# First block of attention: weights left unnormalised, the value product turned round with a ones column, rows scaled, one identity product

## The chip, the cores and the metric

The kernel runs on one core of a Trainium2 chip. The metric is the device time of one execution in microseconds (us). Each core has TensorE (PE in the profile; its weight loads are PEld), VectorE (DVE), ScalarE (ACT), GpSimd (POOL) and SyncE (SP), which issues the transfers. Every engine works through its own instructions in the order in which they were written. SBUF is the working memory, PSUM the memory that TensorE writes its products to.

## What is computed

Sliding-window attention with a linear position bias on 4 batches of 8 heads, 576 positions and 64 elements per head, and behind it two expert layers on the 2304 rows that come out:

```python
scores = scale * np.matmul(q, k.transpose(0, 1, 3, 2))
mask = (rel >= 0) & (rel < window)          # window = 128
scores = np.where(mask, scores + bias[None], -1000000000.0)
scores = scores - np.max(scores, axis=-1, keepdims=True)
attn = np.exp(scores)
attn = attn / (np.sum(attn, axis=-1, keepdims=True) + 1e-09)
attn_out = np.matmul(attn, v)
h = x @ w_in                                 # x: attn_out, 2304 x 512
x = (h * np.clip(h + 3.0, 0.0, 6.0) / 6.0) @ w_out
xn = x / rms * rms_g
out = (silu(xn @ w_gate) * (xn @ w_val)) @ w_out2
```

## The kernel before

The 2304 rows are 18 tiles of 128 rows, taken in six blocks of three. Attention for a block is done two heads at a time: a *pair* is two heads (128 columns of the 512), and a *step* is one pair and one tile of 128 query rows. Block 0 has four pairs of three steps, 12 steps in all. Its attention runs first, on its own, in the loop `for t in range(AHEAD)` (15 turns, called slots below); the attention of the later blocks is woven into the products of the expert layers, and the first three steps of block 1 are begun in slots 12 to 14. Behind the loop comes `product1`, the first product of the first expert layer, with its Relu on ScalarE.

A step consists of these parts, each one slot or more after the one it needs:

- `scores` (S): TensorE, two matmuls (one a head) against up to 256 keys; each float32 matmul shows as two instructions in the trace. The two heads lie on different rows of the array.
- `bias`: VectorE adds the position bias and takes the minimum of each row (the sign is turned), one pass a head.
- `exp`: ScalarE takes the exponential, in `before` with the sum of each row as a second result; GpSimd then adds 1e-9 to the sums and takes the power -1.
- `divide` (D): VectorE multiplies the weights by the reciprocals, one pass a head.
- `transpose` (T): TensorE turns the weights round, 128 keys at a time, into the PSUM tile `ps_t`, which has one buffer. A pair's first step in block 0 has no keys before it and two transposes, the others four.
- `weights`: ScalarE copies `ps_t` to SBUF (`pt`).
- `values` (V): TensorE multiplies with the values as the stationary operand (64 columns, one head) and `pt` as the moving one (128 columns). The heads write to the upper and the lower half of the same PSUM tile `ps_av`, which holds the three steps of a pair and has one buffer.
- `finish`: behind a pair's third step, ScalarE casts `ps_av` into `xs` and VectorE subtracts to get the low part; then the values of the pair two further on are loaded.

`plan` says how many slots behind a pair's first each part of its three steps comes; the table `slots` is filled from it, and the loop takes what `at(t)` gives. The order inside a slot is written out by hand. Between the steps the loop also converts the first two weight tiles from 64-bit words to two 32-bit parts: `W1.step(k, ...)`, whose parts 0, 1 and 4 are ScalarE passes (L131, L136, L145) and 2, 3 and 5 VectorE passes (L140, L143, L147). `prepare` scales the next pair's queries on VectorE and loads the keys and queries of the pair after. Loads are issued by SyncE in the order written.

Of the kernel before, what the change touches and what calls it, by code (L numbers as in the profile page):

```python
# [10 lines left out]
F32 = mybir.dt.float32  # L11
# [4 lines left out]
AF = mybir.ActivationFunctionType  # L16
# [4 lines left out]
P = 128  # L21
# [39 lines left out]
EARLY = {0: 1, 1: 3, 2: 6, 3: 8, M2 - 1: 11}  # L61
PAIRS2 = NTILE // 6

KINDS = "QSDTLV"

OPEN = {"reuse_waits": "tile"}

# [6 lines left out]
def fused_kernel(ctx: ExitStack, tc: tile.TileContext, qd, kd, v, w1, w2, rms_g, out):  # L74
# [201 lines left out]
    class Pair:  # L276
# [17 lines left out]
        def load_v(self):  # L294
            j, k0, nk = self.j, self.lo * P, self.nch * P
            self.vr = ap.tile([P, 4, P], F32, tag="v", name="vraw", bufs=2)
            sp.dma_start(
                out=self.vr[:, : self.nch],
                in_=v[k0 : k0 + nk, j * P : (j + 1) * P].rearrange("(c p) d -> p c d", p=P),
            )  # L300

        def scale(self):
            q = self.qr[:, : self.n * P]
# [26 lines left out]
    class Step:  # L330
# [12 lines left out]
        def scores(self):  # L343
            pr, c0, k0 = self.pair, self.c0, (self.i - 1 - self.pair.lo) * P
            for x, y in PARTS_OF if pr.parts else ():
                for a, s in enumerate(self.s):
                    rows = slice(a * D, (a + 1) * D)
                    pe.matmul(  # L348
                        s[:, c0:],
                        lhsT=pr.qs[rows, x, self.u * P : (self.u + 1) * P],  # L350
                        rhs=pr.ks[rows, y, k0 + c0 : k0 + 2 * P],
                        start=(x == 0 and y == 0),
                        stop=(x == 1),
                    )
            for a, s in enumerate(self.s if not pr.parts else ()):
                rows = slice(a * D, (a + 1) * D)
                pe.matmul(  # L357
                    s[:, c0:],
                    lhsT=pr.qr[rows, self.u * P : (self.u + 1) * P],
                    rhs=pr.kr[rows, k0 + c0 : k0 + 2 * P],  # L360
                    start=True,
                    stop=True,
                )
# [16 lines left out]
                pool.memset(self.t[:, :, :HALF], 0.0)  # L380

        def exp(self):
            self.den = small.tile([P, 2], F32, tag="den", name="den")
            for a in range(2):
                p = self.t[:, a, self.p0 :]
                act.activation(p, p, AF.Exp, bias=self.m[:, a : a + 1], scale=-1.0, accum_out=self.den[:, a : a + 1])  # L386
            self.r = small.tile([P, 2], F32, tag="r", name="r")
            pool.tensor_scalar(self.r, self.den, 1e-9, None, ALU.add)  # L388
            pool.tensor_tensor(self.r, self.r, minus, ALU.pow)  # L389
# [12 lines left out]
        def weights(self):  # L402
# [3 lines left out]
            for c, sign in ((0, -1), (1, 1)) if self.joint else ():  # L406
# [2 lines left out]
                    base=c - 1, pattern=[[0, 2], [sign, P]], channel_multiplier=-sign,  # L409
                )  # L410

        def values(self):
            pr = self.pair
            if pr.acc is None:
                pr.acc = ps_a.tile([P, 3, P], F32, tag="A", name="ps_av")
            for c in range(self.from_, 2):
                for a in range(2):
                    pe.matmul(  # L418
                        pr.acc[a * D : (a + 1) * D, self.u],
                        lhsT=pr.vr[:, self.i - 1 + c - pr.lo, a * D : (a + 1) * D],  # L420
                        rhs=self.pt[:, a, c],
                        start=(c == self.from_),
                        stop=(c == 1),
                        skip_group_check=True,
                    )
# [8 lines left out]
    for k, pr in enumerate(pairs):  # L434
        b, j = divmod(k, H // 2)
        if b < 2:
            t0, plan = 3 * j if b == 0 else AHEAD - 3 + 3 * j, {"S": (0, 1, 2), "D": (1, 2, 3), "T": (2, 3, 4), "V": (3, 4, 5)}
        else:
            t0, plan = AHEAD + M1 * (b - 1) - 2 + 4 * j, {"S": (0, 0, 0), "D": (1, 1, 2), "T": (None, 2, 3), "L": (1, None, None), "V": (5, 5, 5)}
        slots["Q"].setdefault(t0 - (2 if b < 2 else 1), []).append(pr)  # L440
        for u in range(pr.n):
            step = Step(pr, u)
            for kind, at in plan.items():
                if at[u] is not None:
                    slots[kind].setdefault(t0 + at[u], []).append(step)

    def at(t):
        return [slots[kind].get(t, []) for kind in KINDS]

# [125 lines left out]
    busy(WARM)  # L575
    pairs[0].scale()
    for t in range(AHEAD):
        q, s_, d_, t_, _, v_ = at(t)
        scores(s_, t % 2)
        for x in t_:  # L580
            x.transpose()
        for x in v_:
            x.values()
        for x in t_:
            x.weights()
        for x in s_:
            x.bias()
        prepare(q, s_)
        for x in d_:
            x.divide()  # L590
        for x in v_:
            if x.last:
                finish(x.pair)
        for x in s_:
            x.exp()
        if t == 2:
            W1.load(3)
        W1.step(0, *{4: (0,), 5: (1, 2), 7: (3,), 9: (4, 5)}.get(t, ()))
        W1.step(1, *{8: (0,), 11: (1, 2)}.get(t, ()))
# [83 lines left out]
    for p, (b, m0, m1) in enumerate(PARTS):  # L683
# [13 lines left out]
        xs = xs_of[b]  # L697
        for m in range(m0, m1):
            t, slot = slot, slot + 1
            q, s_, d_, t_, l_, v_ = at(t)  # L700
            go = p < 3 or last or (t - AHEAD) % 4 in (0, 3)
            if p == 3 and m == 2:
                first.close()
# [301 lines left out]
```

## Time and profile before

| | before |
|---|---|
| time, median of 3 runs | 956.25 us (955.87 to 956.81) |
| span of the profiled execution | 954.2 us |
| PE busy | 937.7 us (98%) |
| DVE busy | 640.5 us (67%) |
| ACT busy | 454.2 us (48%) |
| POOL busy | 186.3 us (20%) |
| PE tenths in the first four of 40 slices | 7, 8, 9, 9 |
| TensorE clock in the first two slices, tenths of full speed | 8, 9 |

A slice is 23.9 us. The page's chain of work that ended last is 87% PE. The clock is the one that was granted: full is 2.4 GHz, half is 1.2 GHz. In the rows below a group "x4" is four instructions that follow each other; its time is the stretch that they cover, and for a group of one form "mean ns" is that of a single instruction, from its start to its result, so that successive ones overlap.

### The profile page before, as it was taken

The page shows a single profiled execution, that of the slowest core. Times are in us where ns is not written, and L with a number is a line of the kernel's source. Part 1 is how long each engine was busy: PE and PEld are TensorE (multiplying, and loading weights), DVE is VectorE, ACT ScalarE, POOL GpSimd, SP SyncE. Part 2 cuts the span into 40 slices and gives each one's busy share as a digit, 9 for nine tenths or more (in the row PEclk, how much of TensorE's full clock was granted, in tenths as well). Part 3 has the DMA queues.
Part 4 walks back from the last instruction along what each step waited for, and adds up shares of the span by engine and source line. Part 5 has one row for each costly group of instructions (what it writes and reads, how often), then busy time and mean ns, then how long its engine had stood idle before and what let it go on. Part 6 is the DMA issues. An engine that isn't in the chain of part 4 may idle for free.

```text
span 954.2 us, 14654 instructions
## 1 busy us (share of the span) xinstructions
PE 937.7 (98%) x5336; PEld 832.9 (87%) x5336; DVE 640.5 (67%) x1336; ACT 454.2 (48%) x969; POOL 186.3 (20%) x327
## 2 busy tenths in 40 slices
PE   7899999999999999999999999999999999999998
PEld 4587888888888888888899999999999999999996
DVE  5788667555878777877467657777545577545555
ACT  6899566455666655655455453433131323231120
POOL 4333012332223332422124223310000000000000
PEclk8999999999999999999999999999999999999999
DMA  6555401113666555554355757866757555755521
GB/s 231 183 194 194 187 20 51 32 53 117 198 211 203 172 164 174 164 169 130 122 182 210 287 206 293 320 229 234 249 212 281 214 202 199 265 206 211 214 86 67
DMA packets 67432, 175.02 MB, mean 183 GB/s; under 512 B 5024, under 2 KB 41888, under 8 KB 62624
## 3 DMA queue, kind: packets, MB, share of 16 engines
q1 hardware_dynamic: 67360, 174.09, 52.2%
q8 instruction: 42, 0.69, 0.3%
q14 instruction: 30, 0.25, 0.1%
HBM read 130.03 MB, written 44.04 MB: 182 GB/s over the span
## 4 chain that ended last, share of the span: by engine, by line
PE 87%; DVE 6%; ACT 4%; issue 2%; POOL 1%; ACTq 0%; POOLq 0%; DVEq 0%
PE ps_o L497 19%; PE ps_h L484 18%; PE ps_y L892 15%; PE ps_o L845 10%; PE ps_S L845 8%; PE ps_A L845 6%; PE ps_h L845 4%; PE ps_av L418 2%; PE ps_t L400 2%; PE ps_s L357 1%; DVE wx L143 1%; PE ps_s L348 1%; ACT t L386 1%; ACT wx L136 1%; DVE t L371 1%
## 5 line engine op out<-in xcount | busy, mean ns | idle before, releaser
L497 PE MATMUL ps_o<-w,g 128*128 128x512 f32 x864 | 224.0, 402 | 2.1 <-DVE w L147 1.9
L484 PE MATMUL ps_h<-xs,w 128*128 128x384 f32 x1152 | 220.2, 339 | 0.0
L484 PEld LDWEIGHTS ps_h<-xs,w 128*128 128x128 f32 x1152 | 202.4, 188 | 5.8 <-issue 0.2
L497 PEld LDWEIGHTS ps_o<-w,g 128*128 128x128 f32 x864 | 156.2, 188 | 41.1 <-issue 6.3
L892 PE MATMUL ps_y<-wo,g 128*128 128x512 f32 x648 | 150.2, 390 | 0.5 <-DVE g L881 0.5
L892 PEld LDWEIGHTS ps_y<-wo,g 128*128 128x128 f32 x648 | 121.3, 188 | 25.1 <-DVE g L881 0.9
L723 DVE SCALAR_TENSOR_TENSOR t<-t,ps_h 128x384 f32<-128x384 f32 x96 | 53.2, 554 | 98.7 <-ACT t L722 98.6
L722 ACT ACTIVATE t<-ps_h,three 128x384 f32<-128x384 f32 x96 | 55.5, 578 | 84.1 <-PE ps_h L484 80.2
L899 DVE TENSOR_TENSOR y<-y,ps_y 128x512 f32<-128x512 f32 x90 | 61.7, 686 | 35.3 <-PE ps_y L892 35.0
L386 ACT ACTIVATE t<-t,m 128x128 f32<-128x128 f32 (+1 forms) x144 | 61.4, 428 | 29.4 <-DVE t L378 14.2
L728 ACT CAST g<-t 128x384 fp32r<-128x384 f32 x96 | 49.5, 516 | 47.5 <-DVE t L723 46.2
L734 DVE TENSOR_TENSOR g<-t,g 128x384 fp32r<-128x384 f32 x96 | 54.4, 567 | 23.3 <-ACT g L728 23.0
L868 ACT ACTIVATE r<-r 128x384 f32<-128x384 f32 x36 | 19.0, 527 | 105.6 <-DVE r L867 105.6
L845 PE MATMUL ps_o<-S,tw 128*128 128x384 f32 x336 | 66.2, 339 | 0.3 <-DVE t L865 0.3
L388 POOL TENSOR_SCALAR r<-den 128x2 f32<-128x2 f32 x72 | 27.4, 380 | 187.6 <-ACT t L386 186.0
L845 PEld LDWEIGHTS ps_o<-S,tw 128*128 128x128 f32 x336 | 59.3, 188 | 1.4 <-DVE u L856 0.8
L389 POOL TENSOR_TENSOR r<-r,minus 128x2 f32<-128x2 f32 x72 | 56.0, 778 | 6.0
L407 POOL TENSOR_SCALAR_AFFINE_SELECT pt<-pt 128x256 f32<-128x256 f32 x82 | 34.5, 421 | 107.5 <-ACT pt L405 104.5
L853 ACT COPY s<-ps_S 128x384 f32<-128x384 f32 x18 | 8.7, 481 | 86.9 <-PE ps_S L845 86.9
L371 DVE CUSTOM_DVE_ANT_0 t<-ps_s,rel 128x256 f32<-128x256 f32 (+2 forms) x128 | 45.2, 395 | 3.6 <-PE ps_s L357 3.6
L143 DVE SCALAR_TENSOR_TENSOR wx<-wx,wy 128x512 uint32<-128x512 uint32 (+1 forms) x52 | 44.2, 850 | 0.0
L136 ACT ACTIVATE wx<-wraw 128x512 f32<-128x512 f32 (+1 forms) x52 | 42.8, 824 | 0.0
(138 smaller groups left out, 1471.9 us busy)
## 6 DMA issues: line engine op xcount, KB each, us to landing
tw<-t SPq DMA_DIRECT2D x52, 896.0 KB, 6.3
wraw<-w SPq DMA_DIRECT2D x36, 512.0 KB, 4.1
wo<-w SPq DMA_DIRECT2D x18, 1024.0 KB, 4.9
wraw<-w SPq DMA_DIRECT2D x16, 1024.0 KB, 9.1
t<-th SPq DMA_DIRECT2D x12, 896.0 KB, 4.3
t<-tl SPq DMA_DIRECT2D x12, 896.0 KB, 4.3
b<-wx SPq DMA_DIRECT2D x24, 256.0 KB, 2.6
w<-w SPq DMA_DIRECT2D x12, 512.0 KB, 3.0
```

Source lines behind the costliest of these rows:

```text
L143: vec.scalar_tensor_tensor(out=xi, in0=xi, scalar=3, in1=y, op0=ALU.logical_shift_left, op1=ALU.bitwise_or)
L371: vec.tensor_tensor_reduce(out=self.t[:, a, c0:], in0=s[:, c0:], in1=(rel_split if self.i in SPLITS else rel)[:, c0:], scale=2.0 ** (-8.0 ...
L386: act.activation(p, p, AF.Exp, bias=self.m[:, a : a + 1], scale=-1.0, accum_out=self.den[:, a : a + 1])
L389: pool.tensor_tensor(self.r, self.r, minus, ALU.pow)
L484: pe.matmul(ps[:, : n * P], lhsT=w[:, a, c * P : (c + 1) * P], rhs=xs[c][:, b, : n * P], start=(k == 0), stop=(k == 3 * KC - 1),)
L497: pe.matmul(o, lhsT=g[:, a, i * P : (i + 1) * P], rhs=w[:, b], start=(m == first and a == 0 and b == 0), stop=(m == last and a == 1),)
L722: act.activation(r[:, :nq], ps[:, :nq], AF.Relu, bias=three)
L723: vec.scalar_tensor_tensor(out=r[:, :nq], in0=r[:, :nq], scalar=6.0, in1=ps[:, :nq], op0=ALU.min, op1=ALU.mult)
L734: vec.tensor_sub(g[:, 1, :nq], r[:, :nq], f32(g[:, 0, :nq]))
L845: pe.matmul(ps, lhsT=w[a][:, k, c * P : (c + 1) * P], rhs=x[:, b, c], start=(start and j == 0), stop=(j == 5), skip_group_check=True,)
L892: pe.matmul(ps, lhsT=gs[i + k][:, a, t // 3, t % 3 * P : (t % 3 + 1) * P], rhs=wo[i + k][:, b], start=(k == 0 and a == 0 and b == 0), stop ...
L899: vec.tensor_add(acc[t], acc[t], ps)
```

## The change

Only block 0 is changed. Its values are loaded head by head, and each head's 64 columns are followed by a column of ones (`va`), which GpSimd fills. The exponentials have no sums as a second result, GpSimd's two instructions and VectorE's division are not called. The new `rows` takes the transposed weights as the stationary operand and the values with the ones column as the moving one, so that each head gives 128 rows of 64 values and their sum, in a PSUM tile that nothing else uses here (`o2`). VectorE adds 1e-9 to the sums, takes the reciprocal and scales the rows into a tile of `gpool`. One slot later the new `columns` turns both heads of a step round with one identity product into `ps_av`. T comes one slot after S, V (now `rows`) one slot after T, and X (`columns`) where V was. Inside a slot, `columns` comes before the transposes, the weights copy behind the exponentials, and the finish behind both.

```diff
         def load_v(self):
             self.vr = ap.tile([P, 4, P], F32, tag="v", name="vraw", bufs=2)
-            sp.dma_start(
-                out=self.vr[:, : self.nch],
-                in_=v[k0 : k0 + nk, j * P : (j + 1) * P].rearrange("(c p) d -> p c d", p=P),
-            )
+            x = v[k0 : k0 + nk, j * P : (j + 1) * P].rearrange("(c p) d -> p c d", p=P)
+            if self.b:
+                sp.dma_start(out=self.vr[:, : self.nch], in_=x)
+                return
+            self.va = self.vr.rearrange("p c d -> p (c d)")[:, : self.nch * 2 * (D + 1)]
+            self.va = self.va.rearrange("p (c a d) -> p c a d", a=2, d=D + 1)
+            pool.memset(self.va[:, :, :, D:], 1.0)
+            for a in range(2):
+                sp.dma_start(out=self.va[:, :, a, :D], in_=x[:, :, a * D : (a + 1) * D])
...
         def exp(self):
+            if self.pair.b == 0:
+                for a in range(2):
+                    p = self.t[:, a, self.p0 :]
+                    act.activation(p, p, AF.Exp, bias=self.m[:, a : a + 1], scale=-1.0)
+                return
...
+        def rows(self):
+            pr = self.pair
+            ps = ps_out.tile([P, 2, D + 1], F32, tag="o2", name="ps_rows")
+            for a in range(2):
+                for c in range(self.from_, 2):
+                    pe.matmul(
+                        ps[:, a],
+                        lhsT=self.pt[:, a, c],
+                        rhs=pr.va[:, self.i - 1 + c - pr.lo, a],
+                        start=(c == self.from_),
+                        stop=(c == 1),
+                    )
+            r = small.tile([P, 2], F32, tag="r", name="r")
+            vec.tensor_scalar(r, ps[:, :, D], 1e-9, None, ALU.add)
+            vec.reciprocal(r, r)
+            self.x = gpool.tile([P, 2, D], F32, tag="g", name="rows")
+            vec.tensor_tensor(self.x, ps[:, :, :D], r.unsqueeze(2).to_broadcast([P, 2, D]), ALU.mult)
+
+        def columns(self):
+            pr = self.pair
+            if pr.acc is None:
+                pr.acc = ps_a.tile([P, 3, P], F32, tag="A", name="ps_av")
+            pe.transpose(pr.acc[:, self.u], self.x.rearrange("p a d -> p (a d)"), ident)
...
+            if b == 0:
+                plan = {"S": (0, 1, 2), "T": (1, 2, 3), "V": (2, 3, 4), "X": (3, 4, 5)}
...
     for t in range(AHEAD):
-        q, s_, d_, t_, _, v_ = at(t)
+        q, s_, d_, t_, _, v_, x_ = at(t)
         scores(s_, t % 2)
+        for x in x_:
+            x.columns()
         for x in t_:
             x.transpose()
-        for x in v_:
-            x.values()
-        for x in t_:
-            x.weights()
         for x in s_:
             x.bias()
+        for x in v_:
+            x.rows()
         prepare(q, s_)
         for x in d_:
             x.divide()
-        for x in v_:
+        for x in s_:
+            x.exp()
+        for x in t_:
+            x.weights()
+        for x in x_:
             if x.last:
                 finish(x.pair)
-        for x in s_:
-            x.exp()
```

TensorE, slots 5 and 6, where the first pair ends and the second one's first product into `ps_av` follows; before (L357 scores, L400 transposes, L418 values):

```order
L357 MATMUL ps_s_306<-kraw,qraw 128x256
L357 MATMUL ps_s_307<-kraw,qraw 128x256
L400 MATMUL ps_t<-ident,t 128x128 x2
L418 MATMUL ps_av<-pt,vraw 64x128 x4
L357 MATMUL ps_s_343<-kraw,qraw 128x128
L357 MATMUL ps_s_344<-kraw,qraw 128x128
L400 MATMUL ps_t<-ident,t 128x128 x4
L418 MATMUL ps_av<-pt,vraw 64x128 x2
```

and with the change (L362 scores, L445 columns, L410 transposes, L428 rows):

```order
L362 MATMUL ps_s_311<-kraw,qraw 128x256
L362 MATMUL ps_s_312<-kraw,qraw 128x256
L445 MATMUL ps_av<-ident,rows 128x128
L410 MATMUL ps_t<-ident,t 128x128 x4
L428 MATMUL ps_rows<-vraw,pt 128x65 x2
L362 MATMUL ps_s_351<-kraw,qraw 128x128
L362 MATMUL ps_s_352<-kraw,qraw 128x128
L445 MATMUL ps_av<-ident,rows 128x128
L410 MATMUL ps_t<-ident,t 128x128 x4
L428 MATMUL ps_rows<-vraw,pt 128x65 x4
```

The product into `ps_av` was the last thing of a slot and is now the second, right behind the scores; the row products stand last.

VectorE, slots 7 and 8, with the conversion's combining pass between them; before (L371 the minimum passes, L304 the scaling of the queries, L394 the division, L143 the combining pass):

```order
L371 ISA t,m<-ps_s_370,rel 128x256
L371 ISA m 128x1
L304 TENSOR_SCALAR qraw<-qraw,qscale 128x384
L394 TENSOR_SCALAR t<-t,r 128x128 x2
L143 SCALAR_TENSOR_TENSOR wx<-wx,wy 128x1024
L371 ISA t,m<-ps_s_398,rel 128x256
```

and with the change (L376 the minimum passes, L436 to L439 the three instructions of `rows`, L309 the scaling):

```order
L376 ISA t,m<-ps_s_381,rel 128x256
L376 ISA m 128x1
L436 TENSOR_SCALAR r<-ps_rows 128x2
L437 RECIPROCAL r<-r 128x2
L439 TENSOR_TENSOR rows<-ps_rows,r 128x128
L309 TENSOR_SCALAR qraw<-qraw,qscale 128x384
L143 SCALAR_TENSOR_TENSOR wx<-wx,wy 128x1024
L376 ISA t,m<-ps_s_408,rel 128x256
```

The scaling and the combining pass now stand behind three instructions that wait for TensorE's row products of the same slot.

ScalarE, slot 5, with the first pair's finish (L327, then L332, the cast of `ps_av`); before:

```order
L405 COPY pt<-ps_t 128x2x128
L327 CAST xs<-ps_av 128x384
L386 ACTIVATE t,den<-t,m 128x256 x2
L136 ACTIVATE wx<-wraw 128x1024
L405 COPY pt<-ps_t 128x512
```

and with the change:

```order
L391 ACTIVATE t<-t,m 128x256 x2
L415 COPY pt<-ps_t 128x512
L332 CAST xs<-ps_av 128x384
L136 ACTIVATE wx<-wraw 128x1024
L391 ACTIVATE t<-t,m 128x128 x2
```

The exponentials of a slot stood last of its attention work and now stand first; the cast is behind them and behind the weights copy.

## Rows read from the trace of the kernel before

**Rows 1.** Timeline: start us, us, engine line operation tiles, [idle before, releaser].
```profile
8.74 0.67 PE L400 MATMUL ps_t<-ident,t 128*128 128x128 f32 x2 [1.60 <-DVE t L394]
9.34 0.80 PE L357 MATMUL ps_s<-kraw,qraw 64*128 64x128 f32 x4
...
16.89 0.49 PE L357 MATMUL ps_s<-kraw,qraw 64*128 64x128 f32 x4
...
23.26 0.49 PE L357 MATMUL ps_s<-kraw,qraw 64*128 64x128 f32 x4
...
36.93 0.59 PE L357 MATMUL ps_s<-kraw,qraw 64*128 64x192 f32 x4
...
38.90 2.35 PE L484 MATMUL ps_h<-xs,w 128*128 128x384 f32 x12
...
41.29 0.58 ACT L722 ACTIVATE t<-ps_h,three 128x384 f32<-128x384 f32 x1 [0.91 <-PE ps_h L484]
```

**Rows 2.** Waits, 5 to 41 us: who <- whom, us in total, times, longest.
```profile
DVE t L394 <- POOL r L389: 5.9, 10, 1.3
PE ps_t L400 <- DVE t L394: 5.7, 5, 2.4
...
PEld ps_av L418 <- DVE xs L328: 0.6, 2, 0.4
```

**Rows 3.** Stretches: us, busy time of each engine, granted clock, transfers.
```profile
9.00:10.00 1.00, 1.00 (x6) 0.62 (x5) 0.97 (x6) 0.55 (x2) 0.55 (x1) 0.50 0.96 286
20.00:21.00 1.00, 0.90 (x10) 0.76 (x12) 1.00 (x6) 0.93 (x5) 0.16 (x1) 1.00 0.00 0
33.00:34.00 1.00, 1.00 (x8) 0.63 (x6) 1.00 (x3) 1.00 (x3) 0.46 (x1) 0.50 0.69 210
```

**Rows 4.** Timeline of slot 7, TensorE's loads and products.
```profile
20.07 0.42 PEld L400 LDWEIGHTS ps_t<-ident,t 128*128 128x128 f32 x4 [1.28 <-ACT pt L405]
...
20.66 0.42 PEld L418 LDWEIGHTS ps_av<-pt,vraw 128*64 128x64 f32 x8 [0.17 <-issue]
20.66 0.66 PE L418 MATMUL ps_av<-pt,vraw 128*64 128x128 f32 x8
...
21.25 0.70 PE L357 MATMUL ps_s<-kraw,qraw 64*128 64x256 f32 x4
```

**Rows 5.** Groups of VectorE by form: busy us, mean ns, idle before.
```profile
L371 DVE CUSTOM_DVE_ANT_0 t<-ps_s,rel 128x256 f32<-128x256 f32 x96 | 36.6, 420 | 2.0 <-PE ps_s L357 2.0
...
L394 DVE TENSOR_SCALAR t<-t,r 128x128 f32<-128x128 f32 x98 | 22.8, 288 | 1.5 <-POOL r L389 1.5
...
L394 DVE TENSOR_SCALAR t<-t,r 128x256 f32<-128x256 f32 x38 | 11.6, 350 | 4.4 <-POOL r L389 4.4
...
L371 DVE CUSTOM_DVE_ANT_0 t<-ps_s,rel 128x128 f32<-128x128 f32 x16 | 4.0, 286 | 1.6 <-PE ps_s L357 1.6
```

**Rows 6.** Chain that ended last, slots 0 and 1: start us, us, what.
```profile
5.78 0.09 issue
...
6.21 0.89 ACT t L386 x4
...
8.69 0.04 issue
```

**Rows 7.** Timeline of slots 5 to 7, ScalarE and VectorE.
```profile
17.00 0.48 ACT L327 CAST xs<-ps_av 128x384 fp32r<-128x384 f32 x1
...
17.52 0.56 DVE L328 TENSOR_TENSOR xs<-ps_av,xs 128x384 fp32r<-128x384 f32 x1
...
20.82 0.59 ACT L405 COPY pt<-ps_t 128x512 f32<-128x512 f32 x1
...
21.81 0.50 ACT L386 ACTIVATE t<-t,m 128x256 f32<-128x256 f32 x1
...
22.28 1.22 DVE L143 SCALAR_TENSOR_TENSOR wx<-wx,wy 128x1024 uint32<-128x1024 uint32 x1
```

**Rows 8.** Transfers in the first 60 us: count, KB each, median us to landing.
```profile
vraw<-v SPq DMA_DIRECT2D x4, 192.0 KB, 3.5
```

More of the change, by code (lines that the diff above doesn't have):

```diff
@@ L62 @@
 PAIRS2 = NTILE // 6
-KINDS = "QSDTLV"
+KINDS = "QSDTLVX"
 OPEN = {"reuse_waits": "tile"}
@@ L699, in fused_kernel @@
             t, slot = slot, slot + 1
-            q, s_, d_, t_, l_, v_ = at(t)
+            q, s_, d_, t_, l_, v_, _ = at(t)
             go = p < 3 or last or (t - AHEAD) % 4 in (0, 3)
```

## The prediction

> **What bounds the kernel now.** I read the page first: TensorE is busy over nearly the whole span, so the time is its stream of products, and an edit that adds no product can only move the stretches where that stream waits. The tenths by slice put those at the very start. So the rest is read in the first 45 us: the timeline for when each step begins, the waits, the chain of waits, and small windows for the clock.
>
> The first block of attention runs before the first product of the expert layer, in 15 turns of one loop that I call slots (t = 0 to 14). Slot 3 opens at 9.34 (its scores), slot 6 at 16.89, slot 9 at 23.26, slot 14 at 36.93; the first product starts at 38.90 and its Relu at 41.29 [rows 1]. From that Relu on, both ScalarE and VectorE go on with work that queues behind it, and the next Relu follows them; whatever time the Relu moves by, the rest moves by. So the quantity to predict is the Relu's start, now 41.29.
>
> What ends last inside a slot now: VectorE's division waits for GpSimd's reciprocals, 5.9 us in 10 waits, and TensorE's transposes wait for the division, 5.7 us in 5; a pair's finish holds up the next pair's values by only 0.6 us [rows 2]. TensorE's clock is also part of it: it stood 1.60 us ahead of the transposes at 8.74 [rows 1] and 2.4 in its longest wait for a division [rows 2], and after each of these stands the clock is 0.50, that is 1.2 GHz (9 to 10 and 33 to 34 us); around 20 us it is 1.00, 2.4 GHz [rows 3]. Slots 6 to 8, all at the full clock, took 6.37 us.
>
> **The change, part by part.**
>
> GpSimd's two instructions and VectorE's two divisions of each of the 12 steps go, and with them the hand-over that costs 5.9 us. A new ring takes its place. In slot t TensorE now runs scores, then the column transpose of step t-3, then the transposes of step t-1, then the row products of step t-2. The column transpose reads what VectorE made in slot t-1 out of that slot's row products. So each slot contains, in series: row products, hand-over, three VectorE instructions, hand-over, column transpose, transposes, row products again. Only the scores lie beside VectorE's part.
>
> Row products. Today eight value loads, of 64 columns each, keep the weight port busy for 0.42 us, 0.0525 each, and their eight matmuls take 0.66, the two heads side by side [rows 4]. Now the loads are 128 columns wide, so 0.105 each by that row, and the heads no longer share the array. The reads are 65 columns instead of 128. If the loads set the pace, eight cost 0.84 plus a tail of about 0.21 for the last read, 1.05; four cost 0.63. The lower bound is today's 0.66 (0.44 for four, if the loads hide), the upper one is loads and reads in turn, about 1.3. I take 1.05, because the loads alone give 0.84.
>
> By the Trainium skill, TensorEngine Tiling (Array Packing), Performance Considerations, an operand of at most 64 columns should be made the stationary one and two such should share the array, for up to 2x. That speaks against this change, which undoes just that: twice 0.66 would be 1.32, and eight steps at +0.27 with four at +0.13 would put the sum 2.7 us higher. The trace of before shows the sharing, not its absence.
>
> VectorE's three: addition and reciprocal on 128x2, product on 128x128 out of PSUM. No row has 128x2. The 128x256 and 128x128 minimum passes (420 and 286 ns) give 1.05 ns an element and 152 ns at none; the scalings (350 and 288) give 226 at none [rows 5]. So 0.15 to 0.23 for the addition, 0.15 to 0.30 for the reciprocal, whose steps no row shows, and 0.29 for the product. I take 0.18, 0.20, 0.29 and 0.06 between them: 0.73, bounds 0.59 to 0.85. Hand-overs are 0.09 from TensorE to VectorE and 0.04 back, 0.05 with rounding [rows 6]. Together 0.87.
>
> Transposes: four loads in 0.42, so about 0.11 each [rows 4]. With the column transpose, a slot with four has 0.55, one with two 0.33.
>
> The ring per slot, then: eight rows and four transposes 1.05 + 0.87 + 0.55 = 2.47; eight and two 2.25; four and four 0.63 + 0.87 + 0.55 = 2.05. A pair of heads has one of each: 6.77 us, against 6.37 for slots 6 to 8 now.
>
> The finish of a pair. The accumulator has one buffer, so the next pair's first column transpose waits for the finish of the pair before. The finish is now emitted behind the exponentials and the weights copy of its slot, and its reader comes straight behind the scores. From the opening of the slot with a pair's last column: scores 0.70 [rows 4], hand-over 0.09 [rows 6], two minimum passes 0.42 each [rows 5], last exponential 0.50, weights copy 0.59, cast 0.48, subtraction 0.56 [rows 7], and some 0.15 for three hand-overs: 3.9. The ring alone would bring the next column transpose 0.9 us into the slot after, at 2.95. So a pair's end costs 1.0 more. For the second pair VectorE also has a query scaling and the weight conversion's combining pass (1.22) [rows 7] between its ring work of slot 7 and the minimum passes of slot 8; the scores beside them hide little of it, so about 1.3 more, 2.3. The conversion's cast and subtraction in slot 9 cost another 0.5.
>
> The start gains little. The exponentials of step 0 end at 7.10 and the transposes now start at 8.74 [rows 1, 6]; without GpSimd they start near 6.9. But those of step 1 wait for the weights copy of step 0, which now stands behind the exponentials of step 1; slot 3 opens at about 9.1 instead of 9.34.
>
> ScalarE no longer reads out 24 sums; it waits on the ring, so this is worth nothing here. What covers it is that ring; in a slot shorter than 2 us it would count.
>
> The sum. Slot 3 at 9.1; three pairs of 6.77 to slot 12: 29.4; ends of pairs 1.0 + 2.3, conversion 0.5: 33.2. Slot 12 has 2.47 + 1.0 (third pair's end), slot 13 no transposes and 2.1: slot 14 at 38.8. From its opening to the Relu is 4.36 now (36.93 to 41.29). The last cast now stands behind the exponentials and the weights copy of slot 14, whose transposes wait for their division: 2.5 to the copy, 0.59, 0.48, 0.56, then three matmuls, 0.7 with their tail, and hand-overs, 5.1 to 5.3. Relu at 44.1 to 44.2 against 41.29: **+2.9 us**. The profiled span is 954.2 and the median of the runs 956.25, so 2.05 lies outside it; 954.2 + 2.9 + 2.05 = 959.15.
>
> Loads. The value load of each first-block pair is two transfers of 256 B rows: four more issues on SP, ahead of the next keys, queries and weights in its queue, and each first half waits for GpSimd's fill of the ones columns. The third pair's load can go out in slot 5, near 16.5, and such a load lands in about 3.5 [rows 8]; its reader comes near 23. Even twice as long is hidden there, and by the wait at slot 9.
>
> By the Trainium skill, DMA: Bandwidth & Descriptors, Specifications, transfers under 512 B lose line rate. If these took twice as long, the third pair's values would land near 23.5, and the sum would be 0 to 0.5 us higher; no row of before has a large transfer of 256 B rows.
>
> **The rivals.**
>
> *The clock falls in the new waits.* TensorE would stand 2.5 us or so before the column transpose of slot 9, and 1.3 to 1.7 before those of slots 6 and 12. In before the clock was at half after stands of 1.60 and 2.4 [rows 1 to 3]. Against it: the first of these stands goes. Slot 14 was reached from slot 9 in 13.7 us, 2.7 a slot, part of it at half clock, against 2.1 in slots 6 to 8. One such spell adds about 1.5 to the ring, two about 3: 960.6 to 962.5. Chance 0.25.
>
> *The row products stay as cheap as the values.* If wide loads hide behind the reads and eight cost 0.75, the ring loses 0.3 in eight slots and 0.15 in four, hardly anything at the finish waits: 2 us less, 957.1, no change. The loads' own row speaks against it. Chance 0.25.
>
> *Faster.* VectorE's part hides under the scores and the finish gates nothing, as today. This needs three instructions within 0.5 us and cheap row products. Then a pair costs 6.37 + 0.33 = 6.7 or less without any excess, slot 12 opens at 29.7, and three slots at 2.1 bring the first product to 36.2 instead of 38.90: -2.5, so 953.7. The emission order speaks against it: the cast is behind the weights copy in the queue whatever the durations. It decides from a ring under about 2.0 us. Chance 0.13.
>
> **How the numbers follow.** Forecast 0.37, clock 0.25, cheap rows 0.25, faster 0.13. Slower by more than 0.2% (1.9 us, about what a measurement of this kernel can tell from no change) has the first two, 0.62; within 0.25; faster 0.13. The forecast's own range is 957.8 to 960.6 (the ring's terms at their bounds). The range leaves out most of the faster case and the far end of the clock case: 955.6 to 962.6.
>
> **What would show it.** Right: slots of 2.1 to 2.5 us, TensorE's column transposes waiting for VectorE in each, most of all in slots 6, 9 and 12 where the releaser is the finish's subtraction; eight row loads at 0.105 each; Relu near 44.2; no division before slot 13. Wrong: if weight loads of the row products overlap so that eight take 0.75 or less; if the three VectorE instructions take 0.5; if the clock stays at half for longer than it does now, the time is above the forecast; if the Relu moves and the end doesn't, something later has slack that I did not see.

## The result and the profile after

The change made the kernel slower: 966.36 us (median of 4 executions, 963.79 to 971.98) against 956.53, a ratio of 1.0114 with an interval of 1.0083 to 1.0144. Nine more executions beside later experiments gave 961.54 (959.52 to 972.39), 1.0093 (1.0059 to 1.0127). The forecast was 959.2 in a range of 955.6 to 962.6; the sign is right, the first median is 7 us above the forecast and outside the range, and 5 of the 13 executions lie in it.

The page of the profiled execution (span 963.6 us; busy time and share, and the granted clock in tenths by slice of 24.1 us):

```profile
PE 949.8 (99%) x5348; PEld 847.2 (88%) x5348; DVE 641.0 (67%) x1348; ACT 450.7 (47%) x945; POOL 173.4 (18%) x307
...
PEclk8599999999999999999999999999999999999999
```

TensorE is busy for 12 us more than before with about the same work, and the second slice of the clock's row says why: 5 tenths where before had 9. The same in stretches (us, busy time of PE, PEld, DVE, ACT, POOL, granted clock, share of the transfer engines, GB/s):

```profile
5.00:19.00 14.00, 11.10 (x85) 8.56 (x84) 8.60 (x44) 9.97 (x23) 0.11 (x1) 1.00 0.92 322
19.00:50.00 31.00, 29.53 (x124) 23.70 (x124) 16.84 (x69) 15.02 (x37) 3.27 (x8) 0.50 0.25 70
```

From 5 to 19 us TensorE had its full 2.4 GHz; then it had 1.2 GHz for 31 us, through slots 7 to 14 and into the first product, and was busy for 29.5 of them. A stretch at 1.2 GHz is called a spell below, and a wait of TensorE is called a stand. Before had two spells, 6.8 and 3.4 us long by its 1-us windows, of which [rows 3] shows one window each. The timeline around the fall (start, us, engine, line, tiles, and in brackets the idle time before and its releaser; L362 scores, L445 column transposes, L428 row products), and the first Relu:

```profile
17.58 0.30 PE L445 MATMUL ps_av<-ident,rows 128*128 128x128 f32 x1 [1.56 <-DVE xs L333]
...
18.15 1.00 PE L428 MATMUL ps_rows<-vraw,pt 128*128 128x65 f32 x8
19.09 1.22 PE L362 MATMUL ps_s<-kraw,qraw 64*128 64x256 f32 x4
...
20.93 1.80 PE L428 MATMUL ps_rows<-vraw,pt 128*128 128x65 f32 x8
```

```profile
50.72 0.58 ACT L761 ACTIVATE t<-ps_h,three 128x384 f32<-128x384 f32 x1 [2.02 <-PE ps_h L521]
```

Slot 6 has the forecast stand: the column transpose waits 1.56 us for the finish's subtraction. One set of eight row products takes 1.00 us before the fall and 1.80 behind it. The Relu starts at 50.72 against 41.29 [rows 1], 9.43 later, and the span is 9.4 longer (963.6 against 954.2): all of the loss is made before that Relu, and nothing later gives any of it back.

VectorE's part of a slot and its largest wait (5 to 46 us: us in total, times, longest):

```profile
9.14 0.16 DVE L436 TENSOR_SCALAR r<-ps_rows 128x2 f32<-128x2 f32 x1 [0.37 <-PE ps_rows L428]
9.34 0.17 DVE L437 RECIPROCAL r<-r 128x2 f32<-128x2 f32 x1
9.54 0.29 DVE L439 TENSOR_TENSOR rows<-ps_rows,r 128x128 f32<-128x128 f32 x1
```

```profile
DVE r L436 <- PE ps_rows L428: 13.1, 12, 2.7
...
PE ps_av L445 <- DVE xs L333: 2.8, 2, 1.6
```

The waits for GpSimd [rows 2] are gone. VectorE now waits for TensorE's row products in every slot, 13.1 us in all. Half speed makes only a part of that: with wide reads and 3.4 us at half (below) the same wait is still 8.4 us, so most of it is the ring itself.

### The profile page after: what moved, and what is told of

Its sections match the earlier page's. It is cut to its first block, busy times and chain, and to the rows that moved or that the text cites. A ratio compares the mean times of both kernels' runs of the same rounds, so it can differ in the third digit from the quotient of the medians.

```text
span 963.6 us, 14627 instructions
## 1 busy us (share of the span) xinstructions
PE 949.8 (99%) x5348; PEld 847.2 (88%) x5348; DVE 641.0 (67%) x1348; ACT 450.7 (47%) x945; POOL 173.4 (18%) x307
## 4 chain that ended last, share of the span: by engine, by line
PE 87%; DVE 6%; ACT 4%; issue 2%; POOL 0%; ACTq 0%; POOLq 0%; DVEq 0%
PE ps_o L534 18%; PE ps_h L521 18%; PE ps_y L931 15%; PE ps_o L884 10%; PE ps_S L884 8%; PE ps_A L884 6%; PE ps_h L884 4%; PE ps_av L453 2%; PE ps_t L410 2%; PE ps_s L362 2%; PE ps_rows L428 1%; DVE wx L143 1%; ACT wx L136 1%; PE ps_s L353 1%; DVE t L762 1%
## 5 line engine op out<-in xcount | busy, mean ns | idle before, releaser
L396 ACT ACTIVATE t<-t,m 128x128 f32<-128x128 f32 (+2 forms) x120 | 50.0, 418 | 29.7 <-DVE t L383 14.5
L398 POOL TENSOR_SCALAR r<-den 128x2 f32<-128x2 f32 x60 | 23.6, 393 | 191.1 <-ACT t L396 189.5
L399 POOL TENSOR_TENSOR r<-r,minus 128x2 f32<-128x2 f32 x60 | 47.1, 786 | 5.0
L376 DVE CUSTOM_DVE_ANT_0 t<-ps_s,rel 128x256 f32<-128x256 f32 (+2 forms) x128 | 45.1, 394 | 2.9 <-PE ps_s L362 2.7
L143 DVE SCALAR_TENSOR_TENSOR wx<-wx,wy 128x512 uint32<-128x512 uint32 (+1 forms) x52 | 44.1, 848 | 0.0
```

The lines of the kernel that those rows point to most:

```text
L143: vec.scalar_tensor_tensor(out=xi, in0=xi, scalar=3, in1=y, op0=ALU.logical_shift_left, op1=ALU.bitwise_or)
```

## The experiments

Two theories of the 31 us were set up. **A:** the stands before the finish bring the clock down, and they alone matter. **B:** the row products, with loads of 128 columns and reads of only 65, keep the clock down, whatever brought it there. The experiments call `busy(n)`, which is in the kernel: n products of 128x256 that nobody reads (two instructions each; "idle products" below). Each kernel was timed beside runs of the kernel before, whose medians were 956.05 to 956.44.

**The change once more.**

> The changed kernel once more, beside the others on one chip, since its executions differed by 8 us. Theory B: the clock is at half for 15 to 40 us of the first 50 in each, and the executions differ in where this stretch begins, so in its length: 963 to 972, and none near 959.

Measured: 961.54 us (959.52 to 972.39, 9 executions). The lowest has a mean clock of 0.996; four of 961.2 to 961.5 have 0.994; 966.03 has 0.984 and 967.45 has 0.982. The expectation was missed: five of the nine lie below 963, one of them at 959.52, and the profiled one, with 0.994, was at half for only 10 us. Its clock fell in another place:

```profile
9.33 0.49 PE L362 MATMUL ps_s<-kraw,qraw 64*128 64x128 f32 x4
...
11.72 0.70 PE L362 MATMUL ps_s<-kraw,qraw 64*128 64x256 f32 x4
...
13.88 0.70 PE L362 MATMUL ps_s<-kraw,qraw 64*128 64x256 f32 x4
...
15.82 0.49 PE L362 MATMUL ps_s<-kraw,qraw 64*128 64x128 f32 x4
17.88 0.30 PE L445 MATMUL ps_av<-ident,rows 128*128 128x128 f32 x1 [1.56 <-DVE xs L333]
...
19.39 0.70 PE L362 MATMUL ps_s<-kraw,qraw 64*128 64x256 f32 x4
...
26.74 0.37 PE L445 MATMUL ps_av<-ident,rows 128*128 128x128 f32 x1 [2.75 <-DVE xs L333]
...
27.76 1.81 PE L428 MATMUL ps_rows<-vraw,pt 128*128 128x65 f32 x8
```

```profile
27.00:37.00 10.00, 10.00 (x45) 8.09 (x43) 4.74 (x21) 5.43 (x13) 0.00 (x0) 0.50 0.15 45
37.00:47.00 10.00, 8.70 (x57) 6.49 (x55) 6.34 (x28) 5.77 (x18) 3.14 (x7) 1.00 0.46 133
```

```profile
46.37 0.58 ACT L761 ACTIVATE t<-ps_h,three 128x384 f32<-128x384 f32 x1 [1.30 <-PE ps_h L521]
```

The same stand of 1.56 us in slot 6 was followed by a fall in one execution and by none in the other; here the fall came behind the 2.75 us in slot 9, and the spell lasted 10 us. So a fall can follow a stand but need not, and short reads do not always keep the clock down for 31 us: where the spell begins and how long it lasts differ between executions of one kernel, whose times spread over 13 us.

**Wide reads, stands kept.**

```diff
-            ps = ps_out.tile([P, 2, D + 1], F32, tag="o2", name="ps_rows")
+            ps = ps_out.tile([P, 2, 3 * (D + 1)], F32, tag="o2", name="ps_rows")
+            flat, n = ps.rearrange("p a d -> p (a d)"), 2 * (D + 1)
...
-                        ps[:, a],
+                        flat[:, a * n : (a + 1) * n],
                         lhsT=self.pt[:, a, c],
-                        rhs=pr.va[:, self.i - 1 + c - pr.lo, a],
+                        rhs=pr.va[:, self.i - 1 + c - pr.lo].rearrange("p a d -> p (a d)"),
```

> The changed kernel with row products that read 130 columns instead of 65: each head's weights meet the values of both heads, and half of the result is not used. The stands stay where they are. At the full clock this costs little (a read of 130 columns about 0.11 us beside a load of 0.105). Theory A (the stands bring the clock down): the clock falls near 19 us as with the change, Relu near 50, time 965 or more. Rival B (the short reads behind wide loads are what holds the clock at half): the clock does not fall or is back within some us; Relu near 44 to 46, time 959 to 961.

Measured: 960.07 us (959.97 to 960.45, 4 executions), ratio 1.0038 (1.0023 to 1.0053); mean clock 0.998 in all four. Its stretches, and its timeline in slots 9 to 14:

```profile
25.00:30.00 5.00, 2.85 (x15) 2.65 (x17) 1.70 (x9) 4.54 (x9) 0.00 (x0) 0.77 0.24 65
30.00:35.00 5.00, 4.83 (x32) 3.13 (x30) 4.34 (x18) 2.32 (x6) 0.00 (x0) 0.89 0.16 42
```

```profile
27.15 0.30 PE L446 MATMUL ps_av<-ident,rows 128*128 128x128 f32 x1 [2.70 <-DVE xs L333]
27.29 0.64 PE L410 MATMUL ps_t<-ident,t 128*128 128x128 f32 x4
27.72 1.94 PE L429 MATMUL ps_rows<-vraw,pt 128*128 128x130 f32 x8
...
31.29 1.06 PE L429 MATMUL ps_rows<-vraw,pt 128*128 128x130 f32 x8
...
34.28 0.70 PE L362 MATMUL ps_s<-kraw,qraw 64*128 64x256 f32 x4
36.33 0.30 PE L446 MATMUL ps_av<-ident,rows 128*128 128x128 f32 x1 [1.35 <-DVE xs L333]
...
37.90 0.70 PE L362 MATMUL ps_s<-kraw,qraw 64*128 64x256 f32 x4
...
39.96 0.59 PE L362 MATMUL ps_s<-kraw,qraw 64*128 64x192 f32 x4
```

```profile
45.11 0.58 ACT L762 ACTIVATE t<-ps_h,three 128x384 f32<-128x384 f32 x1 [1.30 <-PE ps_h L522]
```

The stands are all there (1.50 in slot 6, 2.70 and 1.35 us), the clock falls behind the 2.70, and it is back 3.4 us later (the two windows are short of 1.00 by 0.23 and 0.11 of 5 us, which at half speed is 2.3 + 1.1). This is theory B's result for the length of a spell; the fall itself is A's. Reading twice as many columns took 0.06 us more for eight (1.06 against 1.00), and the changed kernel got faster by it.

**Idle products in the stands.**

```diff
         scores(s_, t % 2)
+        busy({6: 4, 9: 7, 12: 4}.get(t, 0))
         for x in x_:
             x.columns()
```

> The changed kernel with idle products (128x256, whose result is never read) put behind the scores of slots 6 (four), 9 (seven) and 12 (four), that is, into the three stretches in which TensorE stands before a column transpose that waits for the finish. At the full clock one such product takes about 0.43 us, so they fit into stands of 1.6 to 2.5 us. Theory A (the stands before the finish bring the clock down, and it is the stands alone): the granted clock is 1.00 from slot 6 on, slots take 2.0 to 2.5 us, the Relu starts near 44 and the time is about 959. Rival B (the row products with their wide loads and short reads keep the clock at half, with or without a stand): the clock falls near 19 us all the same and stays at 0.50 for tens of us; the idle products then lengthen three slots, the Relu is at 52 or later and the time at 966 to 973.

Measured: 959.69 us (959.10 to 966.88, 10 executions), ratio 1.0057 (1.0035 to 1.0080). Six lie at 959.1 to 959.8, as A had it, four at 965.2 to 966.9, and the mean clock says 0.999 or 1.0 for all ten. The profiled execution is one of the four (its Relu is the last line):

```profile
7.57 1.23 PE L362 MATMUL ps_s<-kraw,qraw 64*128 64x256 f32 x4
...
17.81 1.23 PE L362 MATMUL ps_s<-kraw,qraw 64*128 64x256 f32 x4
...
21.70 3.78 PE L610 MATMUL warm<-rel 128*128 128x256 f32 x8
...
26.84 0.70 PE L362 MATMUL ps_s<-kraw,qraw 64*128 64x256 f32 x4
...
51.75 0.58 ACT L762 ACTIVATE t<-ps_h,three 128x384 f32<-128x384 f32 x1 [1.30 <-PE ps_h L521]
```

```profile
10.00:15.00 5.00, 4.95 (x24) 4.15 (x23) 1.73 (x10) 1.95 (x5) 0.00 (x0) 1.00 0.97 354
```

and the same window of the first trace of the change:

```profile
10.00:15.00 5.00, 4.71 (x37) 3.77 (x38) 2.87 (x18) 3.42 (x7) 0.11 (x1) 1.00 1.02 410
```

The durations contradict the 1.00 beside them: four score products take 1.23 us up to 18 us and 0.70 from 27 us, and the window from 10 to 15 holds 24 matmuls where the change, truly at full speed there, has 37. TensorE ran at half from its first scores to about 25 us, when the four idle products of slot 6 ended; the trace has no record of a granted clock before its first rise and shows 1.00. So there is a second way to lose: the clock rises late at the start. Behind the rise it did not fall again in this execution, though the row products have their short reads: with the stands filled, B's "with or without a stand" does not hold. The three executions of the change at 972 us, mean clock "1.0", fit this; none of them was profiled, so that part is argued.

**Both together.** The two edits above in one kernel.

> The changed kernel in its own order, with the wide reads (130 columns, half not used) and the idle products in the stands of slots 6, 9 and 12 together. It is to show what the ring and the finish cost with the clock held in every execution. Theory B: the clock is 1.00 from the first slots on, also in the executions in which the idle products alone left it at half to 25 us; Relu at 44 to 44.8 as the forecast's sum had it with nothing for the clock, 959 to 960 with a spread below 1.5 us. If executions of 965 or more remain, the wide reads do not settle the first rise. If the Relu is at 42 or earlier, the ring or the finish was mis-sized and two errors had cancelled.

Measured: 960.10 us (959.56 to 961.25, 6 executions), ratio 1.0034 (1.0022 to 1.0047). No execution of 965 or more is left, but the spread is 1.7 us, not below 1.5. In the profiled one, the slowest of the six, the score products still take 1.23 us at 7.57 and 0.70 from 13.11 on, so the clock rose late here too, near 12 us, but by some 6 us, not 20; from then on it did not fall. Its Relu missed the expectation of 44 to 44.8:

```profile
46.30 0.58 ACT L763 ACTIVATE t<-ps_h,three 128x384 f32<-128x384 f32 x1 [1.30 <-PE ps_h L522]
```

Against the trace above, with idle products too, the Relu is 5.45 us sooner for a rise some 13 us sooner: about 0.4 us for each us of late rise, though the reads differ too. At that price the 6 us account for what the expectation missed. The idle products also lengthen their slots a little (slot 6 takes 3.79 us, 17.32 to 21.11, against 3.57 without).

**The order of before.**

```diff
         scores(s_, t % 2)
-        for x in x_:
-            x.columns()
...
             x.rows()
+        for x in x_:
+            x.columns()
...
-        for x in s_:
-            x.exp()
         for x in t_:
             x.weights()
         for x in x_:
             if x.last:
                 finish(x.pair)
+        for x in s_:
+            x.exp()
```

> The changed kernel with the order inside a slot put back to that of before: the column transposes behind the row products, the weights copy and the finish ahead of the exponentials. The arithmetic is that of the change. The stand before the finish goes, since the column transpose now has the scores, transposes and row products of its slot ahead of it. Theory A: without the stands the clock is 1.00 through the slots, the Relu starts between 39 and 41.5 and the time is 954 to 957. Rival B: the clock is at half for most of 19 to 45 us, the Relu is near 50 and the time near 965.

Measured: 954.76 us (954.44 to 964.36, 10 executions), ratio 1.0001 (0.9979 to 1.0022). Five executions lie at 954.4 to 954.6 with a mean clock of 1.0, as A had it; the others reach 964.4, and three of them (958.3, 959.3, 964.4) have mean clocks of 0.993 to 0.998. So taking the stands before the column transposes away does not hold the clock in every execution, as A needs. In the profiled one, at 954.61, no stand before a column transpose is left, and the Relu comes 1.5 us sooner than before:

```profile
39.76 0.58 ACT L761 ACTIVATE t<-ps_h,three 128x384 f32<-128x384 f32 x1 [0.42 <-PE ps_h L521]
```

**Only the finish earlier.**

```diff
+        for x in x_:
+            if x.last:
+                finish(x.pair)
         for x in s_:
             x.exp()
         for x in t_:
             x.weights()
-        for x in x_:
-            if x.last:
-                finish(x.pair)
```

> The changed kernel with one thing moved: the finish of a pair stands ahead of the exponentials and the weights copy, the rest of the order is that of the change. The stands in slots 6, 9 and 12 get shorter by about 1 us each. Theory A: the clock holds for longer than with the change; if it holds throughout, the Relu is near 41 to 42 and the time near 956. Rival B: the clock falls near 18 to 20 us as with the change and stays at half, the Relu is near 50 and the time near 965.

Measured: 961.71 us (957.44 to 971.62, 10 executions), ratio 1.0077 (1.0039 to 1.0116). Three executions at 957.4 to 957.7 have a mean clock of 0.996; the change's one execution with that clock took 959.52, so the earlier finish saves about 2 us there. Three at 971.3 to 971.6 have a mean clock of "1.0". The profiled one (965.88) has both ways to lose: its scores run at half up to 21 us, and behind the rise the clock falls again after a stand of 1.72 us in slot 9:

```profile
20.97 0.80 PE L362 MATMUL ps_s<-kraw,qraw 64*128 64x128 f32 x4
...
30.20 0.30 PE L445 MATMUL ps_av<-ident,rows 128*128 128x128 f32 x1 [1.72 <-DVE xs L333]
...
33.41 1.81 PE L428 MATMUL ps_rows<-vraw,pt 128*128 128x65 f32 x8
```

That spell lasted 17 us, from 32 to 49. For A against B the times are inconclusive, since their spread covers what either expects; the trace has a long spell behind one stand, with short reads.

**The order of the change on the old arithmetic.** The loop of before, which had the lines without the sign in the order transposes, values, weights, bias, prepare, divide, finish, exponentials:

```diff
         scores(s_, t % 2)
+        for x in v_:
+            x.values()
         for x in t_:
             x.transpose()
...
         for x in d_:
             x.divide()
+        for x in s_:
+            x.exp()
+        for x in t_:
+            x.weights()
         for x in v_:
             if x.last:
                 finish(x.pair)
```

> The kernel before, with the order inside a slot that the change has: values right behind the scores, exponentials ahead of the weights copy, the finish behind both. Its arithmetic is that of before (division, values with 64-column loads, two heads side by side). Its values now wait for the finish in slots 6, 9 and 12, as the column transposes of the change do. Theory B (a stand brings the clock down, and the row products of the change keep it down): stands of 1 to 3 us and a fall of the clock, but the clock is back within 7 us each time, as in before; 957 to 961. Theory A (the stands are enough for the long stretch): the clock stays at half for 15 us or more behind the stand of slot 6; 962 or more.

Measured: 960.00 us (958.93 to 961.84, 4 executions), ratio 1.0044 (1.0029 to 1.0059). The old products now wait too (L418 values, L400 transposes):

```profile
8.94 0.53 PE L400 MATMUL ps_t<-ident,t 128*128 128x128 f32 x2 [1.63 <-DVE t L394]
...
19.78 0.56 PE L418 MATMUL ps_av<-pt,vraw 128*64 128x128 f32 x4 [1.56 <-DVE xs L328]
...
28.02 0.44 PE L418 MATMUL ps_av<-pt,vraw 128*64 128x128 f32 x4 [1.70 <-DVE xs L328]
28.39 0.66 PE L400 MATMUL ps_t<-ident,t 128*128 128x128 f32 x4
...
33.98 1.12 PE L418 MATMUL ps_av<-pt,vraw 128*64 128x128 f32 x8 [2.32 <-ACT pt L405]
```

```profile
35.00:40.00 5.00, 4.66 (x20) 2.31 (x18) 2.61 (x9) 3.36 (x8) 1.47 (x4) 0.50 0.18 52
40.00:45.00 5.00, 5.00 (x33) 3.64 (x32) 2.81 (x13) 2.89 (x10) 1.71 (x5) 0.61 0.14 30
```

The order by itself costs 4 us, without any of the new instructions, and a part of that is the clock's. In this trace, of the slowest of the four (mean clock 0.989), the clock fell behind three of the four stands shown: the 1.63 us that before has too, the 1.56 and the 2.32. It did not fall behind the 1.70 (four transposes at 28.39 take 0.66, full speed). It came back each time, but the last time only in the window from 40 to 45 us (0.61), about 10 us later: longer than the 7 us expected. So short reads are not the only thing under which the clock stays down for a while.

**Idle products in the kernel before.**

```diff
         scores(s_, t % 2)
+        busy({2: 3, 10: 4}.get(t, 0))
         for x in t_:
             x.transpose()
```

> The kernel before, with idle products (128x256, never read) behind the scores of slots 2 (three) and 10 (four), that is, in its two longest stands (1.60 us ahead of 8.74 and 2.37 us ahead of 30.87). It says how long before takes with the clock held, which the change in the order of before has to be compared with. If the clock holds: the two spells at half (6.8 and 3.4 us in the trace of before) go, the Relu starts near 39.5 and the time is 954 to 955; then the 954.5 of the changed arithmetic in the order of before is the clock's gain alone. If the time stays at 956, the arithmetic itself gains about 1.5 us.

Measured: 954.90 us (954.60 to 955.95, 10 executions), ratio 0.9990 (0.9981 to 0.9999). The clock was not held in every execution. In the profiled one, the slowest, it fell near 18.6 us and was back 3.4 us later, and the Relu came at 40.76, not 39.5:

```profile
18.64 0.96 PE L400 MATMUL ps_t<-ident,t 128*128 128x128 f32 x4 [0.90 <-ACT pt L405]
19.52 1.12 PE L418 MATMUL ps_av<-pt,vraw 128*64 128x128 f32 x8
...
40.76 0.58 ACT L723 ACTIVATE t<-ps_h,three 128x384 f32<-128x384 f32 x1 [0.94 <-PE ps_h L484]
```

The lowest five, with a mean clock of 0.999 to 1.0, are 954.60 to 954.79; the change's arithmetic in the order of before gave 954.44 to 954.61 in its best five. The 0.2 us between them is too little to call a gain: at a like clock and in this order the new arithmetic is worth nothing that shows here, and the 1.5 us or so by which those five lie below the kernel before are the clock's.

**The order of before and wide reads.** The two edits of those names in one kernel.

> The changed kernel in the order of before, and with row products that read 130 columns (half of the result is not used). Theory B: with neither the stands nor the short reads the clock is 1.00 from the first slots on in every execution; the wide reads add 0.06 us to eight row products, so 954.6 to 955.3, with a spread of less than 1 us, where the short reads gave 954.4 to 964.4. If the spread stays, it is the first rise of the clock that the reads do not touch.

Measured: 954.98 us (954.57 to 956.03, 10 executions), ratio 0.9991 (0.9981 to 1.0000); mean clock 0.999 to 1.0 in all. The median is where it was expected, the spread is 1.5 us, not below 1. The executions at 958.3, 959.3 and 964.4 that the short reads had in this order have no counterpart. This is the steadiest version of the new arithmetic (its median is 0.2 us above that with short reads), and it ties with the kernel before with idle products.

**Taken together.** Executions more than 3 us above the lowest of their own kernel: 22 of 43 with short reads (the change 8 of 13, idle products 4 of 10, order 3 of 10, finish 7 of 10), none of 20 with wide reads (4, 6 and 10). In the three pairs that differ in the width of the read alone (the change, idle products, order of before) it is 15 of 33 against none of 20; the wide run with idle products was on another chip than the other experiments. So the reads decide how often the long losses come, spells and late rises taken together. Why they matter, by the columns read or by the time that TensorE spends on reads rather than loads, no run here tells. That stands start the spells is shown less firmly: short stands were followed by a fall in some cases and not in others.

## Why the prediction missed, step by step

**The ring was right.** Eight row products were put at 1.05 and took 1.00, four at 0.63 and took 0.56. VectorE's three took 0.69 from first to last (9.14 to 9.83) against 0.73, with 0.17 for the reciprocal where 0.20 was taken. Slots at the full clock in the second trace of the change: 2.39 (9.33 to 11.72), 2.16 and 1.94, against 2.47, 2.25 and 2.05; a pair is 6.49, not 6.77. One of the signs named was off, without harm: eight row loads take 0.97 us, 0.12 each and not 0.105, and little is left behind them, where the prediction had 0.84 and a tail of 0.21:

```profile
10.68 0.97 PEld L428 LDWEIGHTS ps_rows<-vraw,pt 128*128 128x128 f32 x8
```

By the Trainium skill, TensorEngine Tiling (Array Packing), Theoretical Speedup, tiling the array for a dimension of at most 64 gains up to 2x; undoing all of that would have made eight cost 1.32. The trace has 1.00, between that and the 0.66 of before [rows 4]: the loss is about 1.5x.

**The finish was right.** Slot 6 took 3.57 (15.82 to 19.39) against 2.47 + 1.0; the stand in slot 9 was 2.7 to 2.75 against about 2.5; slot 12 took 3.62 with wide reads (34.28 to 37.90) against 3.47. From the opening of slot 14 to the Relu 5.15 (39.96 to 45.11) against 5.1 to 5.3. With the clock nearly held, the sum stands: 960.07 with wide reads, 959.1 to 959.8 in the good executions with idle products, forecast 959.2.

**The loads were right.** Transfers in the first 60 us (KB each, median us to landing):

```profile
vraw<-v SPq DMA_DIRECT2D x8, 96.0 KB, 3.2
```

Half as large, they land in 3.2 us against 3.5 [rows 8]. By the Trainium skill, DMA: Bandwidth & Descriptors, Specifications, transfers under 512 B fall short of line rate; these landings do not show the doubling that the prediction had set beside its sum, nor do they exclude a smaller loss, and no wait of TensorE in these traces ends with them.

**The clock is the step that failed.** The sum put it at nothing: every slot of the change was added up at full speed, while the Relu of before at 41.29, from which the difference was taken, has before's two spells in it. The rival of a falling clock was named, with the right trigger (the stands of slots 6, 9 and 12), but it was given a chance of 0.25 and a price of "about 1.5" for one spell and "about 3" for two.

The runs showed 31 us at half in the first profiled execution and 10 us in the second. What half speed costs behind the first rise can be read from their Relus, 50.72 and 46.37: 0.2 us for each us, and about 44.3 with none, next to the forecast's 44.1 to 44.2. The run with wide reads fits that (45.11 with 3.4 us). So the long spell cost 6.4 us and the shorter one 2. A late first rise costs more, 0.4 us for each us by the two traces with idle products. The rival's price was not too low for spells as short as those of before: 3.4 and 6.8 us would be 0.7 and 1.4.

What failed was the length. It was taken from before, whose spells ended after some 3 and 7 us under its own products; the prediction changed those products and kept the length. "If the clock stays at half for longer than it does now" stands among its signs of being wrong, without a price or a chance. At half speed the slots of the change run without a pause (10.00 us busy of 10 from 27 to 37), and the clock stayed at 1.2 GHz through them.

None of the 13 executions went without a loss to the clock, ten by their mean clocks (0.982 to 0.996) and the three at 972 by their times; the rival, not the forecast, was the common case. The five in the range are there by the length of their spells, which is luck: the profiled one among them had 10 us at half, worth 2 us.

**The order was the other part of the loss, and the prediction had it inside its sum.** With wide reads the change's order took 960.07 and the order of before 954.98; of these 5.1 us the spell of 3.4 us in the first accounts for 0.7, so the order costs about 4.4 at a like clock. On the old arithmetic it costs about 3: the two executions with a mean clock of 0.994 took 958.93 and 959.45, against 956.05 for before, most of it at 0.995 or 0.996. Whether the rest is what the new arithmetic costs in this order, so few executions do not settle. The rival "faster" asked for a finish that gates nothing and gave 953.7; the arithmetic came near that, 954.4 to 954.6, once the order of before was put back. The prediction said that the emission order speaks against it, rightly, and never priced the order apart.

**Slips in the sums.** They decide nothing: from its own terms the Relu comes at 43.9 to 44.1, two spells bring the time to about 962.2 and not 962.5, and three pairs of 6.7 bring slot 12 of "faster" to 29.4 at the latest and not 29.7, so its time to about 953.

## What to carry to other kernels

A stand of TensorE in a stretch without slack is to be priced twice: its own length, and what half speed costs behind it, here 0.2 to 0.4 us for each us. Take the length of a spell from a stretch with the new products, not from the old trace, and from more than one execution. Where each product brings a wide load and a short read, wider reads with an unused half are worth a trial: here 0.06 us for eight bought back 1.5 us in the median and 12 in the worst execution. Price a change of emission order and a change of arithmetic apart: here the order cost 3 to 4 us, and the arithmetic in the old order nothing that shows.

## What the runs showed of the hardware

- TensorE stayed at 1.2 GHz for 31 us while it was busy for 29.5 of them with, among others, products of 128-column loads and 65-column reads. Other executions with these reads were back at 2.4 GHz after 10 and 17 us; the one profiled with reads of 130 in the same order after 3.4 us.
- Stands of 1.5 to 1.7 us at 2.4 GHz were followed by a fall of the clock in five cases and not in four others (the same 1.56 us in slot 6 once each way); the four of 2.3 to 2.75 us were all followed by one. One fall, in the kernel before with idle products, came where no stand was longer than 0.90 us.
- The first rise to 2.4 GHz, near 5 us in the first trace of the change, came near 22 and 25 us in two others with short reads.
- The granted clock of a trace begins with its first rise. Before that the windows and the mean show 1.00, though four score products take 1.23 us instead of 0.70. Where time and mean clock disagree (966.6 us at "1.0"), the durations of one form of product decide.
